# A fused attention and gated convolution kernel: tail emitted by a list schedule, padded tiles, z in halves, the remainder's bank emptied by one copy

## Chip, cores and metric

The kernel runs on one core of a Trainium2 chip. The metric is the device time of one execution in microseconds; the profile comes from one profiled execution. Engines are named as in the profile: PE is TensorE, PEld its weight loads, DVE is VectorE, ACT is ScalarE, POOL is GpSimd, SP is SyncE, which here only issues DMAs.

## Reference

```python
scores = (1.0 / S) * np.matmul(z, z.transpose(0, 2, 1))      # z: 4 x 3136 x 64
attn = np.maximum(scores, 0.0) ** 2
x = u * np.matmul(attn, v)                                   # u, v: 4 x 3136 x 256
h = np.maximum(x @ w_in, 0.0)                                # w_in: 256 x 1024
hp = h padded by one row of zeros at both ends of the sequence
conv_out = sum(conv_w[k] * hp[:, k:k + S, :] for k in range(3))
gate = 1.0 / (1.0 + np.exp(-conv_out))
out = h * gate @ w_out                                       # w_out: 1024 x 256
```

## The kernel before

Four batches are cut into six blocks of 512 rows of the sequence each, 24 blocks in all, and a remainder of 64 rows per batch. A block takes 25 slots; a slot is one chunk of 128 keys. `scores` multiplies za and zb (z and its low part, both as fp32r) into a PSUM bank "s"; ScalarE applies the relu, ScalarE or VectorE squares, ScalarE casts to fp32r (tile ah), VectorE subtracts for the rest (tile al), and that frees the bank. `attend` accumulates ah and al with v into the two banks av0 and av1. Because scores are symmetric, part of them is not computed again: they are written to DRAM as 16-bit halves by `part` and `spill`, fetched transposed and put together on GpSimd by `join` (tiles tp, tj). In every product both operands are split in a high and a low part, and three matmuls are made of one.

While block n is in attention, block n - 1 goes through the second part, one hidden chunk (128 of 1024 hidden columns, 8 chunks a block) at a time: `ffn_in` makes six matmuls from xh and xl into a bank "ph"; ScalarE applies the relu into the SBUF tile hb (three buffers, with two columns of the neighbour block ahead: `ffn_halo`), and multiplies by the first tap; VectorE adds two taps (`ffn_conv`); ScalarE takes the sigmoid, VectorE gates, ScalarE casts to gh, GpSimd subtracts for gl; `ffn_out` makes two triples of matmuls (lines 584 to 586) into o0 and o1. The eight PSUM banks are two "s", two "ph", av0, av1, o0 and o1.

The order of work is a table of slots: `at(slot, class, function)` puts a step into a class of a slot, and a loop over the slots emits them. Every engine then works through its own queue in that order. In the tail, behind the last slot, the last block's eight chunks and the eight chunks of the joined remainder of all batches (256 rows, tile hr, 266 columns with the seams) follow in pairs with fixed offsets (`T_M`, `T_R`, `T_O`, in `last_block`); the last block uses banks "ph" and collects in av0 and av1, the remainder uses "s" and collects in o0 and o1.

The remainder's attention of a batch is made by `rem_fetch`, `rem_join` (GpSimd), `rem_square` (VectorE), `rem_split`, and `rem_attend`, which accumulates into the bank av0 at the head of the batch's last block but one. `rem_evac` empties av0: ScalarE casts it, VectorE subtracts from it; only then av0 is free for the block. z is prepared by `prep_z` for 512 columns at a time: a cast on ScalarE (za), one on VectorE (zb), two subtractions on GpSimd.

Of the kernel before, what the change touches and what calls it, by code (L numbers as in the profile page):

```python
# [55 lines left out]
T_X = 0  # L56
T_O = [1, 1, 1, 2, 2, 2, 3, 3]
T_C = [3, 3, 3, 3, 1, 1, 2, 1, 2]
T_H, T_L = "AAVAAVAA", "GVGVGVGV"
T_M = [0, 2, 4, 6, 8, 10, 12, 14]  # L60
T_R = [1, 3, 5, 7, 9, 11, 13, 15]
T_P, T_E, T_RO = {4: 0, 5: 0, 6: 1, 7: 4}, 5, 6
# [5 lines left out]
def kernel(  # L68
# [90 lines left out]
    def part_z(c, t, hi, lo):  # L159
        (e0, e1), (e2, e3) = hi, lo  # L160
        copy(e0, za[LO, c], t[LO])
        copy(e1, zb[HI, c], t[HI])
        sub(e2, zb[LO, c], t[LO], za[LO, c])
        sub(e3, za[HI, c], t[HI], zb[HI, c])

    def prep_z(q, cast=None):
        c, t = slice(q * NB, min((q + 1) * NB, S)), zst.pop(q)
        g = nc.gpsimd
        part_z(c, t, (cast or nc.scalar, nc.vector), (g, g))
# [314 lines left out]
    def gate_x(blk, eng):  # L484
        t, o = ut[blk], pav.pop(blk)
        nc.vector.scalar_tensor_tensor(
            out=t[:, 0], in0=o[0], scalar=SCALE, in1=t[:, 0], op0=ALU.mult, op1=ALU.mult
        )
        x = wk.tile([P, NB], F32, tag="x1", name="x1", bufs=1)
        nc.scalar.mul(x, o[1], SCALE)  # L490
        eng.tensor_tensor(out=t[:, 1], in0=x, in1=t[:, 1], op=ALU.mult)

    def split_x(blk, engs):
        t = ut.pop(blk)
        xh[blk] = wk.tile([P, DC, NB], F32R, tag="xh", name="xh", bufs=1)
        xl[blk] = wk.tile([P, DC, NB], F32R, tag="xl", name="xl", bufs=1)
        for dc in range(DC):
            nc.scalar.copy(xh[blk][:, dc], t[:, dc])
            sub(engs[dc], xl[blk][:, dc], t[:, dc], xh[blk][:, dc])

# [9 lines left out]
    def ffn_in(blk, f, tag="ph"):  # L510
# [12 lines left out]
    def ffn_halo(blk, f):  # L523
# [5 lines left out]
        t = wk.tile([P, NB + 2], F32, tag="hb", name="hb", bufs=3)  # L529
# [6 lines left out]
    def ffn_relu(blk, f):  # L536
# [4 lines left out]
        nc.scalar.activation(t[:, 2:], p, AF.Relu)  # L541
        b, q = divmod(blk, QB)
        nc.gpsimd.tensor_copy(halo[:, f] if q < QB - 1 else ends[:, f, b], t[:, NB:])  # L543
# [35 lines left out]
    def ffn_out(blk, f, dc, tag="o"):  # L579
        if f == 0 and dc == 0:  # L580
# [11 lines left out]
    def outs(blk):  # L592
        r = ob[blk]
        if blk == "r":
            r = r.rearrange("p a (b n) -> p a b n", b=B)
            return [
                (out[b, :, QB * NB - 1 :].rearrange("(a p) s -> p a s", p=P), r[:, :, b, : RQ + 1]) for b in range(B)
            ]
# [3 lines left out]
        return [(out[b, :, t + a : t + NB].rearrange("(a p) s -> p a s", p=P), r[:, :, a:])]  # L602

    def evac(blk, end=False):
        e = width(blk)
        o = po.pop(blk)
        if blk == "r":
            r = wk.tile([P, DC, RW], F32, tag="ut", name="ob", bufs=1)
        else:
            r = wk.tile([P, DC, NB], F32, tag="ob", name="ob", bufs=1)  # L610
        ob[blk] = r
        for dc in range(DC):
            if end and dc:
                nc.vector.tensor_copy(r[:, dc, :e], o[dc][:, :e])
            else:
                nc.scalar.copy(r[:, dc, :e], o[dc][:, :e])
        if end:
            for dst, src in outs(blk):
                for dc in range(DC):
                    (nc.scalar if dc else nc.sync).dma_start(out=dst[:, dc], in_=src[:, dc])  # L620

    def store(blk):
        for dst, src in outs(blk):
            nc.sync.dma_start(out=dst, in_=src)
# [14 lines left out]
    for q in range(2, QB + 1):  # L639
        s = 4 * q - LA - 3 if q < QB else 4 * QB - LA - 4  # L640
        at(max(s - 4, -LA), POST, load_z, 0, q)
        at(s, POST, prep_z, q)
    at(-3, POST, prep_z, 1)
# [5 lines left out]
    for b in range(1, B):  # L649
        k0 = (b * QB - 1) * NJ  # L650
        for q in range(QB + 1):
# [10 lines left out]
            at(s, POST, prep_z, q)  # L662
# [7 lines left out]

    n = len(RN) - 1
    for b in range(B):
# [11 lines left out]
        at(k5 + 1, PRE, rem_evac)  # L684
        at(k5 + R_T, PE1, rem_turn)
# [12 lines left out]

    for blk in range(NBLK - 1):
# [3 lines left out]
        ahead = blk == NBLK - 2  # L703
        for f in range(FC):
            s = k0 + FS[f]
            at(s, POST, ffn_halo, blk, f)
            at(s, PE1, ffn_in, blk, f)
            at(s + RELU, C_RELU, ffn_relu, blk, f)
            at(s + TAP, C_TAP, ffn_tap, blk, f)
            at(s + ST1, C_ST1, ffn_conv, blk, f, 1)  # L710
            at(s + ST2, C_ST2, ffn_conv, blk, f, 2)
            at(s + SIG, C_SIG, ffn_sig, blk, f)
            at(s + GATE, C_G, ffn_gate, blk, f, G)
            h = s + (GATE if ahead and f >= FC - 2 else GHI)
            at(h, C_HI, ffn_hi, blk, f, A)
            at(h, PE1, ffn_lo, blk, f, G)
            o0, o1 = s + OUT0, s + OUT1
            if ahead and f in T_P:
                o0 = o1 = NS + T_P[f]
            at(o0, PE0, ffn_out, blk, f, 0)  # L720
            at(o1, PE0, ffn_out, blk, f, 1)
        e = NS + T_E if ahead else s + EVAC
        at(e, C_EV, evac, blk)
        at(e + 1, POST, store, blk)

    def last_block():
        blk = NBLK - 1
        at(NS, PRE, gate_x, blk, V)
        at(NS + T_X, T_C[0], split_x, blk, (V, V))
        at(NS - 2, POST, rem_x)  # L730
        jobs = [(NS + T_M[f], blk, f, "ph", "av") for f in range(FC)]
        jobs += [(NS + T_R[f], "r", f, "s", "o") for f in range(FC)]
        for s, w, f, tag, to in sorted(jobs, key=lambda x: x[0]):
            r, t, s1, s2, g, m, h, l = (s + x for x in T_O)
            at(s, POST, ffn_halo, w, f)
            at(s, PE1, ffn_in, w, f, tag)
            at(r, T_C[1], ffn_relu, w, f)
            at(t, T_C[2], ffn_tap, w, f)
            at(s1, T_C[3], ffn_conv, w, f, 1)
            at(s2, T_C[4], ffn_conv, w, f, 2)  # L740
            at(g, T_C[5], ffn_sig, w, f)
            at(m, T_C[6], ffn_gate, w, f, E[T_L[f]])
            at(h, T_C[7], ffn_hi, w, f, E[T_H[f]])
            at(l, T_C[8], ffn_lo, w, f, E[T_L[f]])
            o = s + 4 if w != "r" else max(s + 4, NS + T_RO)
            at(o, PE0, ffn_out, w, f, 0, to)
            at(o, PE0, ffn_out, w, f, 1, to)
            if f == FC - 1:
                at(o, PE1, evac, w, True)

    last_block()
# [5 lines left out]
    with tc.manual_schedule():  # L757
# [11 lines left out]
        rem_picks()  # L769
        nc.sync.dma_start(out=craw.bitcast(U64), in_=conv_w.rearrange("p f k -> p (f k)"))  # L770
        for k in range(-LA, max(ev) + 1):
# [77 lines left out]
```

## Time and profile before

| what | value |
|---|---|
| median of 3 runs | 1627.96 us (1625.5 to 1630.11) |
| profiled execution | 1626.88 us |
| its span in the profile | 1624.8 us |
| PE, DVE, ACT, POOL busy | 97%, 70%, 76%, 68% |

The span is from the first to the last instruction that the profile shows; 2.1 us of the execution lie around it. A share of busy time is a mean over stages with different limits.

### The profile page before, as it was taken

The numbers are of one execution on the slowest core, as the hardware profiler recorded it, in microseconds if no ns is written. First come the engines' busy times: TensorE is split into PE (matmuls) and PEld (weight loads), VectorE is DVE, ScalarE is ACT, GpSimd is POOL, SyncE is SP. The second block draws the span as 40 slices with busy tenths as digits, with TensorE's granted clock in tenths as the row PEclk, the third lists the DMA queues.
The fourth block names the chain that finished last, engine by engine and source line by source line (L and its number), as shares of the span: only waits on it lengthen the run. The fifth ranks groups of instructions, "written<-read, shape, count | busy, mean of one in ns | idle before, by whom it ended". The sixth has DMA issues, their size and how long they took to land.

```text
span 1624.8 us, 22336 instructions
## 1 busy us (share of the span) xinstructions
PE 1578.1 (97%) x6868; PEld 1277.0 (79%) x6868; DVE 1133.4 (70%) x1712; ACT 1232.6 (76%) x2299; POOL 1106.9 (68%) x1320
## 2 busy tenths in 40 slices
PE   7999999999999999999999999999999999999986
PEld 5667888778888888878888888887888888887874
DVE  7787676666777766666777776666677776666566
ACT  7888777778777777868877777777877777786764
POOL 6766557877866766778776676777775666677632
PEclk9999999999999999999999999999999999999999
DMA  4342334545435445446343444454543444545400
GB/s 143 109 129 69 114 84 108 128 99 131 135 88 136 106 89 133 106 114 141 94 139 95 117 119 109 103 122 96 141 134 90 121 91 102 122 102 121 104 20 20
DMA packets 352921, 175.70 MB, mean 108 GB/s; under 512 B 260640, under 2 KB 337440, under 8 KB 352800
## 3 DMA queue, kind: packets, MB, share of 16 engines
q1 hardware_dynamic: 352080, 173.88, 42.4%
q8 instruction: 53, 0.87, 0.2%
q14 instruction: 68, 0.56, 0.1%
q10 hardware_dynamic: 720, 0.40, 0.1%
HBM read 36.59 MB, written 75.24 MB: 69 GB/s over the span
## 4 chain that ended last, share of the span: by engine, by line
PE 80%; ACT 7%; DVE 5%; POOL 4%; issue 3%; DMA 1%; SPq 0%; ACTq 0%; POOLq 0%; DVEq 0%
PE av L380 41%; PE ph L517 5%; PE ph L515 5%; PE ph L516 5%; PE o L586 5%; PE o L584 5%; PE o L585 5%; PE s L288 5%; PE s L289 4%; DVE ph L553 2%; PE av L445 1%; POOL tj L332 1%; ACT t L340 1%; ACT ph L548 1%; DVE al L144 1%
## 5 line engine op out<-in xcount | busy, mean ns | idle before, releaser
L380 PE MATMUL av<-ah,vv 128*128 128x512 f32 x2400 | 742.5, 392 | 6.6 <-DVE ar L144 3.0
L144 DVE TENSOR_TENSOR al<-s,ah 128x512 fp32r<-128x512 f32 x576 | 397.2, 690 | 220.5 <-ACT ah L356 158.5
L380 PEld LDWEIGHTS av<-ah,vv 128*128 128x128 f32 x2400 | 449.5, 188 | 113.5 <-DVE ar L144 4.7
L380 PE MATMUL av<-al,vv 128*128 128x512 f32 x1152 | 451.7, 392 | 3.7 <-DVE al L144 3.4
L351 DVE TENSOR_TENSOR s<-s,t 128x512 f32<-128x512 f32 x345 | 240.6, 697 | 182.2 <-ACT t L340 180.3
L340 ACT ACTIVATE t<-s 128x512 f32<-128x512 f32 x372 | 222.6, 598 | 115.7 <-PE s L289 102.4
L332 POOL COPY tj<-tp 128x1024 uint16<-128x1024 uint16 x228 | 307.9, 1360 | 0.4
L358 ACT CAST ah<-s 128x512 fp32r<-128x512 f32 x372 | 218.8, 588 | 104.6 <-DVE s L351 103.4
L553 DVE SCALAR_TENSOR_TENSOR ph<-hb,cw,ph 128x512 f32<-128x512 f32 x384 | 286.8, 747 | 12.5 <-ACT ph L548 11.9
L144 POOL TENSOR_TENSOR gl<-hb,gh 128x512 fp32r<-128x512 f32 x188 | 243.4, 1294 | 59.2 <-ACT gh L147 54.8
L308 POOL COPY pl<-t 128x1024 uint16<-128x1024 uint16 x248 | 259.1, 1050 | 9.0 <-DMA dq<-pl 8.6
L380 PEld LDWEIGHTS av<-al,vv 128*128 128x128 f32 x1152 | 216.6, 188 | 54.0 <-DVE al L144 9.1
L543 POOL COPY halo<-hb 128x2 f32<-128x2 f32 x160 | 31.5, 197 | 220.8 <-ACT hb L541 219.7
L288 PE MATMUL s<-za 128*128 128x512 f32 x372 | 148.0, 398 | 18.2 <-DVE al L144 12.6
L584 PE MATMUL o<-gh,wol 128*128 128x512 f32 x384 | 153.4, 399 | 3.7 <-ACT gh L147 2.5
L560 ACT ACTIVATE ph<-ph 128x512 f32<-128x512 f32 x200 | 115.6, 578 | 54.6 <-DVE ph L553 48.6
L586 PE MATMUL o<-gl,woh 128*128 128x512 f32 x384 | 153.0, 399 | 4.1 <-POOL gl L144 2.9
L515 PE MATMUL ph<-xh,wih 128*128 128x512 f32 x384 | 150.4, 392 | 2.4 <-DVE hb L567 2.4
L585 PE MATMUL o<-gh,woh 128*128 128x512 f32 x384 | 152.2, 396 | 0.0
L517 PE MATMUL ph<-xl,wih 128*128 128x512 f32 x384 | 150.9, 393 | 1.0 <-DVE xl L144 0.7
L337 ACT ACTIVATE s<-tj 128x512 f32<-128x512 f32 x228 | 136.7, 600 | 18.8 <-POOL tj L332 18.5
L516 PE MATMUL ph<-xh,wil 128*128 128x512 f32 x384 | 150.3, 391 | 0.0
(118 smaller groups left out, 2117.5 us busy)
## 6 DMA issues: line engine op xcount, KB each, us to landing
dq<-pl SPq DMA_DIRECT2D x228, 256.0 KB, 2.4
vst<-in_v_dram SPq DMA_DIRECT2D x48, 256.0 KB, 3.2
ut<-in_u_dram SPq DMA_DIRECT2D x24, 512.0 KB, 4.3
out_dram<-ob SPq DMA_DIRECT2D x19, 512.0 KB, 3.7
st<-in_z_dram SPq DMA_DIRECT2D x24, 256.0 KB, 3.0
tp<-dq SPq DMA_TRANSPOSE x228, 3.5
dq<-pl SPq DMA_DIRECT2D x20, 128.0 KB, 2.5
wr<-in_moe_w_in_dram SPq DMA_DIRECT2D x8, 256.0 KB, 3.1
```

Of the source, the lines that this page charges most:

```text
L144: eng.tensor_tensor(out=out, in0=a, in1=b.bitcast(F32), op=ALU.subtract)
L308: nc.gpsimd.tensor_copy(pl[k], rl.pop(k).bitcast(U16).rearrange("p (n h) -> p h n", h=2))
L332: nc.gpsimd.tensor_copy(tj[k].bitcast(U16).rearrange("p (n h) -> p h n", h=2), t)
L340: nc.scalar.activation(rl[k], sc[k][:, :NB], AF.Relu, scale=SC1)
L351: nc.vector.tensor_tensor(out=s, in0=s, in1=rl[k], op=ALU.mult)
L380: nc.tensor.matmul(o, lhsT=w[:, j, d], rhs=r, start=first and i == 0, stop=last and i == len(ops) - 1)
L515: nc.tensor.matmul(o, lhsT=wih[:, dc, w], rhs=xh[blk][:, dc], start=(dc == 0), stop=False)
L517: nc.tensor.matmul(o, lhsT=wih[:, dc, w], rhs=xl[blk][:, dc], start=False, stop=(dc == DC - 1))
L553: nc.vector.scalar_tensor_tensor(out=c, in0=hb[blk, f][:, k : e + k], scalar=cw[:, f, k : k + 1], in1=c, op0=ALU.mult, op1=ALU.add,)
L584: nc.tensor.matmul(o, lhsT=wol[:, f, d], rhs=h, start=(f == 0), stop=False)
L585: nc.tensor.matmul(o, lhsT=woh[:, f, d], rhs=h, start=False, stop=False)
L586: nc.tensor.matmul(o, lhsT=woh[:, f, d], rhs=l, start=False, stop=(f == FC - 1))
```

## The change

- The tail (`tail`, in place of `last_block`) is a list of operations with fixed costs and dependencies, ordered by a list schedule and then emitted in that order. The last steps of the block before (chunks 4 to 7) are part of the list. Chunks alternate between banks "s" and "ph" in pairs, all casts are on ScalarE, the subtractions of the last block on GpSimd, those of the remainder on VectorE. Both halves of the last gate are on VectorE. The remainder is stored with one DMA per half instead of four.
- The tile hb has 528 words a row instead of 514. In the program's layout the three buffers of hb stood 2,080 bytes apart, 6,240 in all, so that gh and gl behind them began at 205,536 and 211,680, which is 32 past a multiple of 64. Now the buffers stand 2,112 bytes apart, and gh and gl begin at 199,488 and 205,632, multiples of 64. The tiles ah, al, xh, xl, za and vv begin at multiples of 64 in both.
- `prep_z` has two halves (za cast and its subtraction; zb cast and its subtraction). From the second batch on the second half is two slots later. The zb cast is on ScalarE for odd chunks of columns.
- `rem_evac` copies av0 to an SBUF tile on ScalarE and casts from there; the subtraction (`rem_low`) is on GpSimd, four slots later. `rem_square` is on ScalarE.
- The matrix `pick` (`rem_picks`) is made at slot 100 instead of ahead of the loop. `ffn_in` takes the two matmuls with xl last.

```diff
-    def prep_z(q, cast=None):
-        c, t = slice(q * NB, min((q + 1) * NB, S)), zst.pop(q)
+    def prep_z(q, half):
...
+        if half == 0:
+            copy(nc.scalar, za[LO, c], t[LO])
+            sub(g, zb[LO, c], t[LO], za[LO, c])
+            return
+        copy(nc.scalar if q % 2 else nc.vector, zb[HI, c], t[HI])
+        sub(g, za[HI, c], t[HI], zb[HI, c])
...
     def rem_square(i):
         t = rs[i]
-        nc.vector.scalar_tensor_tensor(out=t, in0=t, scalar=1.0 / SC1, in1=t, op0=ALU.mult, op1=ALU.mult)
+        nc.scalar.activation(t, t, AF.Square, scale=SC1**-0.5)
...
-        nc.scalar.copy(h, o)
-        sub(nc.vector, l, o, h)
+        rr["t"] = t = wk.tile([P, NB], F32, tag="t", name="re", bufs=3)
+        nc.scalar.copy(t, o)
+        nc.scalar.copy(h, t)
+
+    def rem_low():
+        sub(nc.gpsimd, rr["l"], rr.pop("t"), rr["h"])
...
             nc.tensor.matmul(o, lhsT=wil[:, dc, w], rhs=xh[blk][:, dc], start=False, stop=False)
+        for dc in range(DC):
             nc.tensor.matmul(o, lhsT=wih[:, dc, w], rhs=xl[blk][:, dc], start=False, stop=(dc == DC - 1))
...
-        t = wk.tile([P, NB + 2], F32, tag="hb", name="hb", bufs=3)
+        t = wk.tile([P, NB + 16], F32, tag="hb", name="hb", bufs=3)
...
+            at(s, POST, prep_z, q, 0)
+            at(s + 2, POST, prep_z, q, 1)
...
+    at(4 * NJ, POST, rem_picks)
...
+        at(k5 + 5, POST, rem_low)
...
+        def ffn(w, f, stage, x, tag, eh, el, to):
+            n, r = width(w), w == "r"
+            a, v = 90 + 0.82 * n, 60 + 1.07 * n
...
+                d = op("P", 2.5 * (n + 32), x + hold(tag, 2), ffn_in, w, f, tag)
+                d = op("A", a, [d, d0], ffn_relu, w, f)
...
+                d = op("A", a + 100, [d], ffn_tap, w, f)
+                d = op("V", v, [d], ffn_conv, w, f, 1)
+                d = op("V", v + 100, [d], ffn_conv, w, f, 2)
...
+        free, done, order = defaultdict(float), {}, []
+        while len(order) < len(ops):
...
+                t = max([free[e]] + [done[d] + 35 for d in deps])
+                k = (t, -rank[i])
...
+        for i in order:
+            ops[i][3](*ops[i][4])
```

On ScalarE in the tail, before: two pairs of the last block (hb, 512 columns) and the remainder (hr, 256 or 266 columns). L541 and L539 are the relu, L548 the tap, L560 the sigmoid, L147 the cast; the number behind ph is that of the chunk's bank tile.

```order
L541 ACTIVATE hb_16802<-ph_16810 128x512
L548 ACTIVATE ph_16810<-hb_16802,cw_73 128x512
L560 ACTIVATE ph_16810<-ph_16810 128x512
L539 ACTIVATE hr_16828<-ph_16837 128x4x64
L548 ACTIVATE ph_16837<-hr_16828,cw_73 128x266
L147 CAST gh_16869<-hb_16802 128x512
L560 ACTIVATE ph_16837<-ph_16837 128x266
L541 ACTIVATE hb_16854<-ph_16862 128x512
```

The same engine in the tail after the change, where L552 and L550 are the relu, L562 the tap, L574 the sigmoid, L144 the cast.

```order
L552 ACTIVATE hb_16621<-ph_16664 128x512
L550 ACTIVATE hr_16640<-ph_16678 128x4x64
L562 ACTIVATE ph_16664<-hb_16621,cw_73 128x512
L562 ACTIVATE ph_16678<-hr_16640,cw_73 128x266
L574 ACTIVATE ph_16643<-ph_16643 128x266
L144 CAST gh_16710<-hb_16593 128x512
L552 ACTIVATE hb_16686<-ph_16699 128x512
L574 ACTIVATE ph_16664<-ph_16664 128x512
L562 ACTIVATE ph_16699<-hb_16686,cw_73 128x512
```

Before, the sigmoid of a chunk stands right behind its tap. After, four rows of other chunks stand between the tap and the sigmoid of ph_16664.

On GpSimd, ahead of the second batch, before: two chunks of z (za, zb) among joins (tj), subtractions for gl and halo copies.

```order
L543 COPY halo<-hb 128x2
L144 TENSOR_TENSOR zb<-st,za 64x512
L144 TENSOR_TENSOR za<-st,zb 64x512
L144 TENSOR_TENSOR zb<-st,za 64x512
L144 TENSOR_TENSOR za<-st,zb 64x512
L332 COPY tj<-tp 128x2x512
L144 TENSOR_TENSOR gl<-hb,gh 128x512
```

The same place after the change.

```order
L557 COPY halo<-hb 128x2
L141 TENSOR_TENSOR zb<-st,za 64x512 x2
L328 COPY tj<-tp 128x2x512
L141 TENSOR_TENSOR gl<-hb,gh 128x512
L544 COPY hb<-halo 128x2
L328 COPY tj<-tp 128x2x512
L141 TENSOR_TENSOR za<-st,zb 64x512 x2
```

Two of the four subtractions have moved behind the next two joins.

## Rows read from the trace of the kernel before

**Rows 1.** Windows: busy us (instructions) of PE, PEld, DVE, ACT, POOL; clock; DMA.

```profile
60.00:1559.00 1499.00, 1481.35 (x6461) 1204.99 (x6461) 1045.64 (x1568) 1151.69 (x2134) 1046.86 (x1226) 1.00 0.44 111
1559.00:1625.00 66.00, 47.86 (x224) 36.48 (x222) 40.56 (x70) 35.70 (x73) 15.92 (x45) 0.95 0.07 21
```

**Rows 2.** The chain that ended last, one pair of the tail: start, us, what.

```profile
1593.03 0.70 ACT ph L548
...
1593.76 0.77 DVE ph L553
...
1595.34 0.58 ACT ph L560
...
1596.31 0.50 ACT ph L548
...
1598.87 0.70 ACT ph L548
```

**Rows 3.** Groups of the tail (1559:1625): busy us, mean ns, idle before, its releasers.

```profile
L560 ACT ACTIVATE ph<-ph 128x512 f32<-128x512 f32 x10 | 5.8, 580 | 11.6 <-DVE ph L553 11.6
...
L553 DVE SCALAR_TENSOR_TENSOR ph<-hb,cw,ph 128x512 f32<-128x512 f32 x18 | 13.5, 754 | 9.9 <-ACT ph L548 9.7
...
L144 POOL TENSOR_TENSOR gl<-hb,gh 128x512 fp32r<-128x512 f32 x7 | 8.9, 1278 | 16.5 <-ACT gh L147 12.2 <-DVE gh L147 4.3
```

**Rows 4.** Timeline of PE, two stretches of the tail: start, us, instruction.

```profile
1559.23 0.39 PE L515 MATMUL ph<-xh,wih 128*128 128x512 f32 x1
...
1560.59 0.40 PE L584 MATMUL o<-gh,wol 128*128 128x512 f32 x1
...
1563.41 0.40 PE L515 MATMUL ph<-xh,wih 128*128 128x512 f32 x1
...
1608.64 0.28 PE L515 MATMUL ph<-xr,wih 128*128 128x256 f32 x1
...
1609.23 0.28 PE L517 MATMUL ph<-xr,wih 128*128 128x256 f32 x1
```

**Rows 5.** Timeline of the end, PE's last matmul and SP's last issues.

```profile
1618.40 0.28 PE L586 MATMUL o<-al,woh 128*128 128x266 f32 x1
...
1617.92 3.38 SPq L620 DMA_DIRECT2D out_dram<-ob  x5
```

**Rows 6.** DMA issues of the end: KB each, median us to landing.

```profile
out_dram<-ob SPq DMA_DIRECT2D x4, 32.5 KB, 2.4
```

**Rows 7.** Waits of PE, 60:1559: us in total, times, longest us.

```profile
PE s L288 <- DVE al L144: 12.6, 11, 2.8
PE av L380 <- DVE ar L144: 3.0, 4, 0.8
```

**Rows 8.** Timeline where the remainder's bank is emptied, second batch: ACT, DVE, PE.

```profile
727.73 0.59 ACT L456 CAST ar<-av 128x512 fp32r<-128x512 f32 x1 [5.31 <-PE av L445]
...
728.35 0.69 DVE L144 TENSOR_TENSOR ar<-av,ar 128x512 fp32r<-128x512 f32 x1 [6.12 <-ACT ar L456]
...
729.09 0.50 PE L380 MATMUL av<-ah,vv 128*128 128x512 f32 x1 [0.75 <-DVE ar L144]
```

**Rows 9.** Timeline of POOL and PE, z prepared ahead of the second batch.

```profile
279.48 1.29 POOL L144 TENSOR_TENSOR zb<-st,za 64x512 fp32r<-64x512 f32 x1 [1.16 <-DVE zb L147]
...
284.92 1.34 POOL L332 COPY tj<-tp 128x1024 uint16<-128x1024 uint16 x1
...
288.70 0.50 PE L288 MATMUL s<-za 128*128 128x512 f32 x1 [2.39 <-DVE al L144]
```

**Rows 10.** Timeline of DVE and PE, squares of the first batch's remainder.

```profile
318.22 1.74 DVE L431 SCALAR_TENSOR_TENSOR rj<-rj 128x512 f32<-128x512 f32 x1 [2.51 <-POOL rj L410]
...
326.18 0.50 PE L288 MATMUL s<-za 128*128 128x512 f32 x1 [2.79 <-DVE al L144]
```

**Rows 11.** Timeline of DVE and PE at the start.

```profile
8.12 1.24 DVE L394 CAST pick<-pk 128x64 fp32r<-128x64 f32 x1 [2.11 <-POOL pk L391]
...
10.74 0.77 PE L380 MATMUL av<-ah,vv 128*128 128x512 f32 x1 [1.81 <-ACT ah L358]
```

More of the change, by code (lines that the diff above doesn't have):

```diff
@@ L157, in load_z @@
         zst[q] = t[:, :w]
[L159 to L164, printed above, removed]
-    def prep_z(q, cast=None):
-        c, t = slice(q * NB, min((q + 1) * NB, S)), zst.pop(q)
-        g = nc.gpsimd
-        part_z(c, t, (cast or nc.scalar, nc.vector), (g, g))
+    def prep_z(q, half):
+        c = slice(q * NB, min((q + 1) * NB, S))
+        t = zst.pop(q) if half else zst[q]
+        g = nc.gpsimd
+        if half == 0:
[4 more added lines that the diff above has]
+        sub(g, za[HI, c], t[HI], zb[HI, c])
         if q == QB:
@@ L540, in ffn_relu, with ffn_keep @@
             return
-        nc.scalar.activation(t[:, 2:], p, AF.Relu)
+        nc.scalar.activation(t[:, 2 : NB + 2], p, AF.Relu)
+    def ffn_keep(blk, f):
+        t = hb[blk, f]
         b, q = divmod(blk, QB)
-        nc.gpsimd.tensor_copy(halo[:, f] if q < QB - 1 else ends[:, f, b], t[:, NB:])
+        nc.gpsimd.tensor_copy(halo[:, f] if q < QB - 1 else ends[:, f, b], t[:, NB : NB + 2])
     def ffn_tap(blk, f):
@@ L579, in ffn_out @@
     def ffn_out(blk, f, dc, tag="o"):
-        if f == 0 and dc == 0:
+        if blk not in po:
             po[blk] = [ps.tile([P, 512], F32, tag=f"{tag}{i}", name=f"o{i}") for i in range(DC)]
@@ L601, in outs, with evac, store_half @@
         t = q * NB - 1
-        return [(out[b, :, t + a : t + NB].rearrange("(a p) s -> p a s", p=P), r[:, :, a:])]
-    def evac(blk, end=False):
+        return out[b, :, t + a : t + NB].rearrange("(a p) s -> p a s", p=P), ob[blk][:, :, a:]
+    def evac(blk, dcs=range(DC), engs=(nc.scalar, nc.scalar)):
         e = width(blk)
-        o = po.pop(blk)
-        if blk == "r":
[L608 to L620, printed above, removed]
+        if blk not in ob:
+            if blk == "r":
+                ob[blk] = wk.tile([P, DC, RW], F32, tag="ut", name="ob", bufs=1)
+            else:
+                ob[blk] = wk.tile([P, DC, NB], F32, tag="ob", name="ob", bufs=1)
+        for dc in dcs:
+            copy(engs[dc], ob[blk][:, dc, :e], po[blk][dc][:, :e])
+    def store_half(blk, dc, eng):
+        if blk == "r":
+            dst = out[:, dc * P : (dc + 1) * P, QB * NB - 1 :].rearrange("b p s -> p b s")
+            eng.dma_start(out=dst, in_=ob[blk][:, dc].rearrange("p (b n) -> p b n", b=B)[:, :, : RQ + 1])
+            return
+        dst, src = outs(blk)
+        eng.dma_start(out=dst[:, dc], in_=src[:, dc])
     def store(blk):
-        for dst, src in outs(blk):
-            nc.sync.dma_start(out=dst, in_=src)
+        dst, src = outs(blk)
+        nc.sync.dma_start(out=dst, in_=src)
     ev = defaultdict(lambda: tuple([] for _ in range(6)))
@@ L697, with before_end @@
         at(blk * NJ + 6, POST, load_u, blk)
+    def before_end(slot, *args):
+        if slot < NS:
+            at(slot, *args)
     for blk in range(NBLK - 1):
@@ L702 @@
         at(k0 + XS, C_XS, split_x, blk, (G, G))
-        ahead = blk == NBLK - 2
         for f in range(FC):
             s = k0 + FS[f]
+            if s == NS - 1:
+                break
             at(s, POST, ffn_halo, blk, f)
@@ L711 @@
             at(s + ST2, C_ST2, ffn_conv, blk, f, 2)
[L712 to L749, printed above, removed]
@@ L768 @@
         prep_v(0, V)
-        rem_picks()
         nc.sync.dma_start(out=craw.bitcast(U64), in_=conv_w.rearrange("p f k -> p (f k)"))
-        for k in range(-LA, max(ev) + 1):
+        for k in range(-LA, NS):
             e = ev[k]
@@ L807 @@
                 run(e[PE1])
+        tail()
 _INS = ['u', 'v', 'z', 'moe_w_in', 'moe_conv_w', 'moe_w_out']
```

132 lines of the change are left out of this document (107 added, 25 removed).

## Prediction

> **What bounds the kernel now.** I read the stages first. From 60 to 1559 us TensorE is busy 1481.35 of 1499 us, while ScalarE, VectorE and GpSimd are busy about 70 to 77% [rows 1]. So the body runs at TensorE's own rate, and an edit there counts only where TensorE waits or where its matmuls get shorter. After the last attention matmul, at about 1559.0, the picture changes: in 66 us TensorE works 47.86, VectorE 40.56 and ScalarE 35.70 [rows 1]. Nothing is full, so the tail is bound by order. The chain of waits shows which: one pair (a chunk of the last block, then a chunk of the remainder) runs from 1593.03 to 1598.87, 5.84 us, through ScalarE's tap, two convolution steps on VectorE, the sigmoid, then the same for the remainder, and only then the next tap [rows 2]. The groups of the tail say the same: ScalarE waits 11.6 us in front of the sigmoid for VectorE, VectorE waits 9.9 us in front of the convolution for ScalarE [rows 3]. The two engines take turns.
>
> The profiled execution took 1626.88 us, 1.1 below the median of the three; I make the sum against it.
>
> **The tail's order.** In the new order ScalarE has two or three rows of other chunks between a tap and the sigmoid that waits for VectorE behind it, so the turns overlap. What remains is the largest load. For TensorE I count it: 54 matmuls of 512 columns into the hidden chunks at 0.227 us (six in 1.36 us, [rows 4]) are 12.3 us; 72 out of them, at 0.235 now (twelve in 2.82 us, [rows 4]) and 0.227 if the next part holds, are 16.9 or 16.3; 48 of 256 columns at 0.118 (five steps in 0.59 us, [rows 4]) are 5.7; 48 of 266 columns, by columns 0.123, are 5.9. Sum 40.2. ScalarE takes four casts more, at most 0.6 each like the one in [rows 8], and stays under 38.1; VectorE gives those up and trades four subtractions of 512 columns for four of 266, so it is below its 40.56; GpSimd has some ten subtractions of 1.28 us [rows 3]. So TensorE becomes the bound, with VectorE close behind. A slot of PSUM does not hold it up: a chunk of the last block may start when the second one before it is gated, and 1.36 + 0.58 + 0.70 + 2 x 0.77 + 0.58 + 0.70 = 5.5 us [rows 2] (relu and gate taken like the sigmoid and the tap) for two pairs is 2.8 a pair against TensorE's 4.2 (two sets of 1.4, one of 0.7, one of 0.74). Waits are left: the end (the last remainder chunk has some 4 us of elementwise work, of which the outputs of the two last chunks and of two remainder chunks, 4.3 us, cover most) and places where the tail's in-order queues meet VectorE late. Between nothing and 8 us (one more microsecond a pair) I take 3.
>
> Behind the last matmul the end took 1624.8 - 1618.40 = 6.4 us. Four small stores per half become one: SyncE's five issues took 3.38 us, 0.68 each [rows 5], and one of the small stores landed 2.4 us after its issue [rows 6]. One issue in place of four saves up to 2.0 on that queue; as the joined store has four times the pieces I take back a little and count 1.6 saved, 4.8 left. The tail then ends at 1559.0 + 40.2 + 3.0 + 4.8 = 1607.0 instead of 1624.8: **-17.8 us** (-12 with the 8 us of waits and a store that gains nothing, -20 with 1 us of waits).
>
> **The padded tiles.** The triple that multiplies by the output weights steps at 0.235 us, the triple ahead of it at 0.227, both with 512 columns, 128 rows and the same clock [rows 4]. What differs is where the moving tile lies: only gh and gl begin 32 bytes past a multiple of 64; after the padding they begin on one. [...] That the address is the cause is inferred from two groups of rows, no run here shows it yet. 1152 such matmuls, less the 72 already counted, times 0.0075 to 0.008 are 8.1 to 8.6 us of a body in which TensorE is 99% busy. Some will come back as waits, since others must keep up: I take **-7**, between 0 and -8.6.
> The Trainium skill's page "TensorE: Matmul & The Clock Gate", section "Back-to-back issue gap", speaks against this edit: it gives the spacing of warm matmuls as columns / 2.4 + 2.5 ns, 215.8 ns for 512, with no term for an address. By that page the padding changes nothing. Neither of the two spacings in the rows is the page's, and they differ from each other, so I go by the rows.
>
> **The remainder's bank.** Four times, once a batch, TensorE waits for the accumulator of the remainder, 3.0 us in all [rows 7]. ScalarE copies it at 727.73 for 0.59, then VectorE subtracts at 728.35 for 0.69, and the matmul starts at 729.09 [rows 8]. After the change the bank is free when the copy ends, 728.32, so it starts about 0.7 earlier. ScalarE then has one more cast (0.59) in front of the next attention cast, which was needed only after two matmuls and an output triple. 4 x 0.6 = **-2.4** (bounds -0.4 and -3.0). The subtraction moves to GpSimd four slots later, ahead of the turn at slot 13, which leaves it several slots.
>
> **z in halves and the squares.** The other waits of the body are those of the scores for VectorE's subtraction, which frees their bank: 12.6 us in 11 places [rows 7]. Two have a cause that the change touches. At 279.48 four z subtractions of 1.29 stand in a row on GpSimd ahead of a join at 284.92, and TensorE then waits 2.39 at 288.70 [rows 9]; in the new order two stand there and two behind the next two joins. That is 2.7 us less ahead of the first join, so the wait can go whole; I take 2.0, as the other pair now delays a later join. At 318.22 VectorE's square waits 2.51 for GpSimd and then takes 1.74; TensorE waits 2.79 at 326.18 [rows 10]. On ScalarE the nearest row, a copy of 512 columns, is 0.59 [rows 8], so 1.15 is gained and VectorE is no longer held behind that wait; but ScalarE is now held instead. I take 2.0 over all four batches (bounds +2 and -4). The zb casts that go to ScalarE (odd chunks) lie in its idle 23%; they would cost where it is already late. Together **-4** (bounds 0 and -6.4).
>
> **The start.** VectorE waits 2.11 for the pick matrix and spends 1.24 on it at 8.12, and the first attention matmul starts at 10.74 after a wait for what comes behind it [rows 11]. That work moves to slot 100, long before the matrix is first used. ScalarE gets one cast of z more there (0.6 at most). 1.81 of wait, less that: **-1.2** (bounds 0 and -1.8).
>
> **At nothing:** the order of the six input matmuls (the first of them in a block waits for its tile, the others have it), the second gate half on VectorE, the earlier list positions of halo copies.
>
> Sum: 17.8 + 7 + 2.4 + 4 + 1.2 = 32.4, so 1626.9 - 32.4 = **1594.5 us**, 2.0% faster. With the parts at their better and worse ends together about 1588 to 1603; that is this case's own range.
>
> **Rivals.** *The address is not the cause.* Then the spacing of the output triples stays 0.235: -7 and the 0.5 in the tail fall away, 1602 us. For it: no row shows the same tile at another address, and by the page above this is what should come out. Against it: ah, al, xh, xl and za all step at 0.227, and the two groups of rows have nothing else apart but weights that are laid out alike.
>
> *The tail stays a chain.* The new order was made with fixed costs per operation; if one engine is late, every in-order queue behind it is, and when TensorE waits long its clock may be granted at half, as the mean of 0.95 for the tail hints [rows 1]. At 5.3 us a pair in place of 5.84 and the shorter end, the tail gains about 6 us: 1626.9 - 6 - 14.6 = 1606 us. Against it: in the new order no pair of rows that wait for each other stand next to each other on ScalarE until the last chunks.
>
> *Squares that hold ScalarE.* Sixteen squares now stand in ScalarE's queue, each behind a join on GpSimd; behind it wait the relu, the casts and so every engine. VectorE's wait at 318.22 was 2.51 [rows 10]. If each of the sixteen held TensorE for that long, it would cost 40 us and the kernel would end at 1626.9 - 30.4 + 40 = 1637, slower. It decides from 30.4 / 16 = 1.9 us a square. Against it: the body's eleven waits of this kind come to 12.6 us in all, so most of the sixteen joins were not late; joins are also relieved of z work.
>
> **Chances.** The sum as worked out 0.62; the address not the cause 0.18; the tail a chain 0.15; squares that decide 0.05. A difference of 0.3%, about 5 us, is what this kernel's runs can tell from none. The first three are all faster; I leave 0.93 for faster, 0.02 for the same and 0.05 for slower, as the three could meet. For 8 in 10 the range goes from 1588 to 1607, which takes in the two middle rivals.
>
> **What would show it.** Right: output triples at 0.227 in the body; the four waits for the remainder gone to 0.1 or so; no wait of over 1 us at the place of 288.70; in the tail TensorE busy nearly throughout at full clock, from the last attention matmul to the last output in some 43 us; first attention matmul near 9.5. Wrong: triples still at 0.235; ScalarE waiting for GpSimd in front of the squares with the scores late behind it; pairs in the tail over 5 us apart with ScalarE and VectorE still waiting for each other.

## The result and the profile after

The changed kernel takes 1600.25 us (median of 4 runs, 1598.48 to 1600.64), the kernel before 1628.47 us: ratio 0.9827, 95% interval 0.981 to 0.9844. The forecast was 1594.5 us with a range of 1588 to 1607. The profiled execution took 1600.44 us, its span is 1598.67; before it was 1626.88 and 1624.85. The sums by place below are made with the profiled executions, 26.2 us of span apart.

Two rows of the windows of after (window, its length, busy us and count of PE, PEld, DVE, ACT, POOL; granted clock; share and GB/s of the DMA), cut at the last attention matmul, answer to [rows 1]:

```profile
60.00:1552.00 1492.00, 1483.13 (x6455) 1202.93 (x6454) 1017.13 (x1538) 1164.25 (x2161) 1044.36 (x1231) 1.00 0.45 111
1552.00:1599.00 47.00, 41.62 (x222) 34.87 (x221) 35.06 (x66) 34.71 (x75) 17.93 (x45) 0.98 0.09 29
```

The body takes 7.4 us less: the last attention matmul starts at 1551.60 where it started at 1559.01. Of that, 2.4 us are won up to the first attention matmul of the third block (136.56 in place of 138.99) and 5.0 behind it. The tail behind it goes from 65.8 us to 47.07 (1551.60 to the span's end at 1598.67), with TensorE busy 41.62 of it.

**The tail's order.** The first and the last of the sixteen taps (eight chunks of the last block, eight of the remainder) in ScalarE's timeline (start, us, instruction), in before and then in after, answer to the pairs of [rows 2]:

```profile
1566.71 0.69 ACT L548 ACTIVATE ph<-hb,cw 128x512 f32<-128x512 f32 x1
...
1614.49 0.49 ACT L548 ACTIVATE ph<-hr,cw 128x266 f32<-128x266 f32 x1
```

```profile
1558.46 0.69 ACT L562 ACTIVATE ph<-hb,cw 128x512 f32<-128x512 f32 x1
...
1588.95 0.49 ACT L562 ACTIVATE ph<-hr,cw 128x266 f32<-128x266 f32 x1
```

The eight pairs took 47.8 us, 6.0 each; here they take 30.5, 3.8 each. The two kinds of chunk no longer alternate strictly, so only this mean can be compared. The groups of the tail in after (busy us, mean ns of one, idle time before and who ended it) answer to [rows 3]:

```profile
L567 DVE SCALAR_TENSOR_TENSOR ph<-hb,cw,ph 128x512 f32<-128x512 f32 x18 | 13.5, 752 | 3.3 <-ACT ph L562 3.0
...
L574 ACT ACTIVATE ph<-ph 128x512 f32<-128x512 f32 x9 | 5.2, 581 | 2.3 <-DVE ph L567 2.2
```

ScalarE's 11.6 us of waiting in front of the sigmoid are 2.3, VectorE's 9.9 in front of the convolution 3.3: the two no longer take turns. The end in after, its last matmul and SyncE's first store there, then the row of the DMA issues for one half of the remainder's output (KB, us to landing), answers to [rows 5, 6]:

```profile
1591.43 0.34 SPq L628 DMA_DIRECT2D out_dram<-ob  x1
...
1593.82 0.28 PE L600 MATMUL o<-al,woh 128*128 128x266 f32 x1
```

```profile
out_dram<-ob SPq DMA_DIRECT2D x1, 130.0 KB, 2.3
```

From the last matmul to the end it is 4.85 us, 6.45 before.

**The body's waits.** The waits of PE in after from 60 to 1552 us (total, times, longest) answer to [rows 7]:

```profile
PE s L284 <- DVE al L141: 5.6, 7, 1.8
...
PE ph L528 <- POOL xl L141: 0.8, 4, 0.2
```

The scores' waits fell from 12.6 to 5.6 us. The four waits for the remainder's bank are gone from the list, and four others stand in it that were not there.

The timeline of after where the bank is emptied answers to [rows 8]:

```profile
720.92 0.59 ACT L453 COPY re<-av 128x512 f32<-128x512 f32 x1 [5.31 <-PE av L441]
721.54 0.62 ACT L454 CAST ar<-re 128x512 fp32r<-128x512 f32 x1
721.56 0.30 PEld L376 LDWEIGHTS av<-ah,vv 128*128 128x128 f32 x2 [0.45 <-ACT re L453]
...
724.25 1.14 ACT L144 CAST xh<-ut 128x512 fp32r<-128x512 f32 x2
724.94 2.54 POOL L141 TENSOR_TENSOR xl<-ut,xh 128x512 fp32r<-128x512 f32 x2 [8.24 <-ACT xh L144]
...
727.53 0.50 PE L528 MATMUL ph<-xl,wih 128*128 128x512 f32 x1 [0.20 <-POOL xl L141]
```

The bank is free at 721.51 and the matmul goes on at once. (This is the head of the sixth and last block of a batch, where the remainder's attention stands, and not of the last but one.) But the second cast on ScalarE, 0.62, stands ahead of the cast of xh, then GpSimd makes xl, and the second of the hidden chunk's matmuls with xl waits for that.

**z and the squares.** The timeline of after at the places of [rows 9, 10]:

```profile
277.39 2.55 POOL L141 TENSOR_TENSOR zb<-st,za 64x512 fp32r<-64x512 f32 x2 [1.16 <-ACT za L144]
279.87 1.35 POOL L328 COPY tj<-tp 128x1024 uint16<-128x1024 uint16 x1
...
284.14 2.54 POOL L141 TENSOR_TENSOR za<-st,zb 64x512 fp32r<-64x512 f32 x2
...
284.68 0.50 PE L284 MATMUL s<-za 128*128 128x512 f32 x1 [0.41 <-DVE al L141]
```

The wait of 2.39 is 0.41; the one of 2.79 at 326.18 has no successor. The block in which both lie (the fifth, from its first attention matmul to that of the sixth) takes 67.7 us, 72.7 before: 5.0 gained.

**The output triples.** One triple and the matmuls behind it (a row x2 holds two), in after and then in before, answer to [rows 4]; the last row of each is the tenth matmul:

```profile
600.88 0.39 PE L598 MATMUL o<-gh,wol 128*128 128x512 f32 x1
601.11 0.39 PE L599 MATMUL o<-gh,woh 128*128 128x512 f32 x1
601.34 0.39 PE L600 MATMUL o<-gl,woh 128*128 128x512 f32 x1
601.58 0.62 PE L376 MATMUL av<-ah,vv 128*128 128x512 f32 x2
...
602.96 0.62 PE L376 MATMUL av<-ah,vv 128*128 128x512 f32 x2
```

```profile
599.53 0.40 PE L584 MATMUL o<-gh,wol 128*128 128x512 f32 x1
...
601.61 0.39 PE L288 MATMUL s<-za 128*128 128x512 f32 x1
```

The triple steps at 0.233, not at 0.227, and the matmuls behind it are slow too: nine take 2.08 us, where 9 x 0.227 is 2.04. In before the nine took 2.08 as well. Averaged over the nines without a wait from 150 to 1535 us they take 2.075 us in before and 2.080 in after. Nothing came of the padding.

### The profile page after: what moved, and what is told of

The parts are those of the page before. It is cut to its first block, busy times and chain, and to the rows that moved or that the text cites. A ratio compares the mean times of both kernels' runs of the same rounds, so it can differ in the third digit from the quotient of the medians.

```text
span 1598.7 us, 22354 instructions
## 1 busy us (share of the span) xinstructions
PE 1576.5 (99%) x6868; PEld 1275.3 (80%) x6868; DVE 1098.3 (69%) x1676; ACT 1247.7 (78%) x2334; POOL 1108.2 (69%) x1324
## 4 chain that ended last, share of the span: by engine, by line
PE 85%; ACT 6%; DVE 4%; POOL 3%; issue 2%; DMA 0%; POOLq 0%; DVEq 0%; ACTq 0%
PE av L376 43%; PE o L600 5%; PE o L599 5%; PE o L598 5%; PE ph L528 5%; PE ph L525 5%; PE ph L526 5%; PE s L284 5%; PE s L285 5%; PE av L441 1%; POOL tj L328 1%; POOL xl L141 1%; ACT t L336 1%; DVE ph L567 1%; DVE al L141 1%
## 5 line engine op out<-in xcount | busy, mean ns | idle before, releaser
L141 POOL TENSOR_TENSOR gl<-hb,gh 128x512 fp32r<-128x512 f32 x192 | 248.5, 1294 | 55.0 <-ACT gh L144 54.5
L285 PE MATMUL s<-za,zb 128*128 128x512 f32 x372 | 146.4, 393 | 0.0
L552 ACT ACTIVATE hb<-ph 128x512 f32<-128x512 f32 x192 | 114.6, 597 | 37.8 <-PE ph L528 37.1
```

Source lines behind the costliest of these rows:

```text
L141: eng.tensor_tensor(out=out, in0=a, in1=b.bitcast(F32), op=ALU.subtract)
```

## The experiments

Times are medians, to be held against 1600.25 of after. In one place the clock disturbs comparisons of 1 or 2 us: in after it was granted at half, the lower level (1.2 GHz), for 3.4 us from 95.4 us on, behind a wait of 1.81; in *old_evac* (below), with the same wait at 94.73, it was not. The row of each:

```profile
95.40:99.00 3.60, 3.55 (x9) 2.80 (x10) 3.28 (x7) 1.44 (x3) 1.02 (x2) 0.53 0.55 152
```

```profile
94.40:98.00 3.60, 3.27 (x14) 2.71 (x15) 3.37 (x7) 2.50 (x6) 1.74 (x4) 1.00 0.51 152
```

From the second block's first attention matmul to the third's that makes 1.6 us (72.2 and 70.6 us). The profiled executions of after, before, unpadded, operands, low_tiles, squares_dve and picks_early have it, the others not, and after's median holds it, as by their mean clocks three of its four runs do. So where it matters I compare the stretch from the third block's first attention matmul to the last attention matmul, 1415.0 us in after; of these profiles only operands and z_whole have a half clock inside it.

**old_tail**: the kernel after, with the old tail (the slots of its table, its emptying of the banks and its stores).

```diff
...
-    tail()
+    last_block()
```

> All edits of the change except the tail: the tail of before stands behind the new body. If the tail's gain is its own (66 us shrank to 47 after the last attention matmul), this kernel loses about 18.8 us against the changed one, some 1619 us, and its body, from the start to the last attention matmul, is as long as that of the changed kernel, 1551.6 us in the span. If the rival holds, that the new body brings the tail's engines to the end in a better state, the old tail is shorter here than 65.8 us and the kernel ends near 1610.

Measured: 1618.36 us, 0.9947 of before (0.9932 to 0.9962). The new tail is worth 18.1 us, as the prediction's term; by the profiles the tail behind the last attention matmul is 65.30 us here and 47.07 in after, 18.2 apart. The old tail is nearly as long as in before, 65.84, so the new body does not shorten it. The body ends 2.0 us earlier than after's, for the most part since the half clock at 95 us is lacking.

**unpadded**: hb of 514 words again.

```diff
-        t = wk.tile([P, NB + 16], F32, tag="hb", name="hb", bufs=3)
+        t = wk.tile([P, NB + 2], F32, tag="hb", name="hb", bufs=3)
```

> The changed kernel with hb of 514 words again, so that gh and gl lie 32 past a multiple of 64. My term for the padding says 7 us slower, 1607, with output triples 8 ns a matmul longer than those of the changed kernel. The rival, read from the trace of the changed kernel (its triples still step at 0.233 us, and attention matmuls behind them are longer by 1 to 3 ns than before), says that the padding is worth nothing or a small loss: 1597 to 1602, triples at 0.235.

Measured: 1598.05 us (1596.55 to 1599.48), span 1597.4 against 1598.7. The padding wins nothing; by the profiles, with the same half clock in both, it loses 1.3. The nine matmuls show why: 2.075 us here on average, 2.080 in after, and there are 384 of them, up to 2 us in all.

**operands**: the triples of the first output half take other weights, those of the second half z as their moving tile.

```diff
...
+        if blk != "r" and dc == 0:
+            wa, wb = wil[:, 0, f * P : (f + 1) * P], wih[:, 0, f * P : (f + 1) * P]
+        if blk != "r" and dc == 1:
+            h, l = za[:, :NB], za[:, NB : 2 * NB]
...
```

> The changed kernel with other operands in the output triples, so the output is not the reference's: for the first half of the columns the weights are taken from the input weights, for the second half the moving tile is z. It asks what makes output triples step at 0.233 us where all other matmuls of 512 columns step at 0.227. If it is the address or the content of the moving tiles gh and gl, the first half stays at 0.233 and the second falls to 0.227. If it is the weights' place, the first half falls and the second stays. If it is the PSUM bank, both stay.

Measured: 1601.35 us in one run. Its timeline, a triple of each half:

```profile
602.09 0.39 PE L603 MATMUL o<-gh,wil 128*128 128x512 f32 x1
...
604.17 0.39 PE L284 MATMUL s<-za 128*128 128x512 f32 x1
...
604.62 0.39 PE L603 MATMUL o<-za,wol 128*128 128x512 f32 x1
...
606.66 0.62 PE L376 MATMUL av<-ah,vv 128*128 128x512 f32 x2
```

Nine matmuls from a triple on take 2.08 us with gh and other weights, 2.04 with z and the old weights. So it is the moving tile, neither the weights nor the bank, and the slow steps of the attention matmuls behind it go with it. In the blocks where z is prepared that gain is lost: in the fifth the triples wait 3.1 us for the writing of za, with a stretch of half clock from 277.1 us on, so it gains 0.7 us on before, where after's gains 5.0, and in the ninth and the fifteenth they wait 0.9 each. The other 19 blocks from the third on take 5.0 us less than in after: half the triples, and half of what *in_phase* (below) gains there.

**low_tiles**: gh and gl at another place.

```diff
+        for n in ("gh", "gl"):
+            nc.vector.memset(wk.tile([P, NB], F32R, tag=n, name=n, bufs=3)[:, 0:1].bitcast(F32), 0.0)
         load_z(0, 0)
```

> The kernel after the change, but the six tiles of gh and gl are set aside first of the work pool, so that they lie at byte 128832 to 141119 of a partition in place of 199488 to 211775; what came before them moves up by 12 KB, with xh at 197248 and xl at 201344, inside the old range. If the place in SBUF makes the slow steps, the output triples go from 0.233 us to 0.227 and the six matmuls behind them from 1.381 to 1.362; xl, now where gh was, may go to 0.233. Then 384 triples gain 0.038 us each, 14 us, less 384 x 0.006 for xl: 1588 us. If what the tiles hold makes it, the triples stay at 0.233, xl at 0.227, and the time stays at 1600.

Measured: 1600.6 us, the nine still 2.08. Not the place as such; but the new address is as far past a multiple of 512 bytes as the old one (320), which I saw only later.

**plain_data**: other contents in gh and gl of all blocks, not in the remainder's.

```diff
-        copy(eng, g[0], cc[blk, f])
+        if blk == "r":
+            copy(eng, g[0], cc[blk, f])
+        else:
+            copy(eng, g[0], wih[:, 0, :NB].bitcast(F32))
```

> The kernel after the change, but the cast into gh reads 512 columns of the input weights in place of the gated chunk, so that gh and gl hold numbers of the size of the weights (some 0.06) and not those of the hidden chunk; the output is not the reference's. Instructions, addresses and waits stay. If what the tiles hold makes the slow steps, the output triples go to 0.227 us and the attention matmuls behind them to 0.227 as well, and the kernel to about 1586. If the place makes them, all steps stay as they are, at 1600.

Measured: 1598.55 us in one run, without the half clock at 95 us; a triple and the tenth matmul:

```profile
599.29 0.39 PE L601 MATMUL o<-gh,wol 128*128 128x512 f32 x1
...
601.37 0.62 PE L376 MATMUL av<-ah,vv 128*128 128x512 f32 x2
```

The nine take 2.08 us with numbers of another size: not the contents.

**align128**: hb of 544 words.

```diff
-        t = wk.tile([P, NB + 16], F32, tag="hb", name="hb", bufs=3)
+        t = wk.tile([P, NB + 32], F32, tag="hb", name="hb", bufs=3)
```

> The kernel after the change, with hb tiles of 544 words in place of 528, so that gh and gl begin on a multiple of 128 bytes; after the change they begin 64 bytes past one, before it 96 bytes past one, and so they still did in the run with gh and gl at a low place. All other moving tiles (ah, al, xh, xl, za) begin on a multiple of 128, and they step at 0.227 us. If the address within 128 bytes makes the slow steps, the output triples go to 0.227 us and the six attention matmuls behind each to 1.362 from 1.381: 384 times 0.038 us, 14 us less, 1586. If not, and only the sort of tile or its writers count, 1600.

Measured: 1598.54 us (1598.49 to 1601.21), no gain beyond the half clock, which its profiled execution lacks. The steps moved, though:

```profile
598.73 0.40 PE L598 MATMUL o<-gh,wol 128*128 128x512 f32 x1
598.97 0.39 PE L599 MATMUL o<-gh,woh 128*128 128x512 f32 x1
599.19 0.40 PE L600 MATMUL o<-gl,woh 128*128 128x512 f32 x1
...
600.81 0.62 PE L376 MATMUL av<-ah,vv 128*128 128x512 f32 x2
```

On average the triple steps at 0.234, 0.225 and 0.237 in place of three times 0.233, and the nine are 2.08 as ever. The address shapes how the loss is spread, and a multiple of 128 is not the cure.

**shift_ah**: 64 bytes ahead of all that follows ah.

```diff
...
+            zst["pad"] = wk.tile([P, 16], F32, tag="pad", name="pad", bufs=1)
...
         ah[k] = wk.tile([P, NB], F32R, tag="ah", name="ah", bufs=4)
```

> The kernel after the change, with 64 bytes set aside ahead of the ring of ah, so that all that comes after it moves up by 64 bytes: ah, al, xh and xl then begin 64 bytes past a multiple of 128, gh and gl on one. If the address within 128 bytes makes the slow steps, the output triples go to 0.227 us and the attention matmuls, the hidden chunks' matmuls go to about 0.233: some 5300 attention matmuls of 512 columns and 1150 of the hidden chunks lose 0.006 us each, 39 us, less 14, so 1625. If not, all steps stay as they are, 1600.

Measured: 1611.78 us in one run, 11.5 slower than after; without the early half clock, from the third block to the last attention matmul, 1428.3 us against 1415.0, 13.2 slower. From 150 to 1540 us the attention matmuls step at 0.232 on average and the hidden chunks' at 0.230. (The trace has 3552 attention matmuls, not the 5300 of the expectation, whose 39 us become 28.) The scores' matmuls, whose tile za had not moved, went from 0.227 to 0.237 and 0.229, and the triples, though on a multiple of 128 now, stayed slow; as slow steps run on for some five matmuls, both could come from the tiles ahead of them.

One reading is that a tile is slow only beside tiles that begin at another offset. The long runs of attention matmuls speak against it. Nine matmuls in the midst of 18 that read ah and al alone, here and then in after:

```profile
323.25 0.63 PE L380 MATMUL av<-ah,vv 128*128 128x512 f32 x2
...
325.36 0.40 PE L529 MATMUL ph<-xh,wih 128*128 128x512 f32 x1
```

```profile
323.75 0.61 PE L376 MATMUL av<-ah,vv 128*128 128x512 f32 x2
...
325.79 0.39 PE L525 MATMUL ph<-xh,wih 128*128 128x512 f32 x1
```

They take 2.11 us here and 2.04 in after. All these tiles have one offset in either kernel; in after the steps are back at 0.227 from the sixth matmul of such a run on, here they are still 0.232 at the eighteenth (means of 16 runs). And the 25 matmuls of a batch's remainder that read vv, set aside with za and not moved, are back at 0.227 from the sixth on in this kernel too. So a common offset is not enough: the offset itself counts. By the addresses of the compiled programs, bytes past a multiple of 512:

| kernel | za | ah, al, xh, xl | gh, gl | nine matmuls, us |
|---|---|---|---|---|
| before, unpadded | 128 | 128 | 224 | 2.08 |
| after, plain_data, low_tiles | 128 | 128 | 320 | 2.08 |
| align128 | 128 | 128 | 0 | 2.08 |
| shift_ah | 128 | 192 | 384 | 2.09 |
| operands, second half | 128 | 128 | za in their place | 2.04 |

**in_phase**: gh and gl set aside in hi_half, behind xl, so that they too begin 128 past a multiple of 512.

```diff
+        if blk == 0 and dc == 0:
+            for n in ("gh", "gl"):
+                nc.gpsimd.memset(wk.tile([P, NB], F32R, tag=n, name=n, bufs=3)[:, 0:1].bitcast(F32), 0.0)
```

> The kernel after the change, but the rings of gh and gl are set aside right behind xl, ahead of hb, so that gh begins at byte 193152, which is 128 past a multiple of 512, as are the beginnings of all moving tiles that step at 0.227 us (za 16512, ah 156288, al, xh, xl). In the kernel after the change gh begins 320 past such a multiple, in the run with the low place 320 too, in before 224 and in the run with tiles of 544 words 0, and in each of these an output triple and the six matmuls behind it took 2.075 to 2.080 us in place of 9 x 0.227 = 2.043. If the phase of the address within 256 or 512 bytes makes it, all nine go to 0.227, and 384 times 0.037 us are won: 14 us, 1586. If another thing of gh and gl makes it (that they are newly written, their ring), the nine stay at 2.08 and the time at 1600.

Measured: 1586.95 us (1586.26 to 1588.58, 5 runs), 0.9756 of before (0.9742 to 0.9769). It beats both kernels. A triple, and the next triple nine matmuls on:

```profile
600.64 0.39 PE L601 MATMUL o<-gh,wol 128*128 128x512 f32 x1
600.87 0.39 PE L602 MATMUL o<-gh,woh 128*128 128x512 f32 x1
601.10 0.39 PE L603 MATMUL o<-gl,woh 128*128 128x512 f32 x1
601.32 0.61 PE L376 MATMUL av<-ah,vv 128*128 128x512 f32 x2
...
602.68 0.39 PE L601 MATMUL o<-gh,wol 128*128 128x512 f32 x1
```

All nine step at 0.227, 2.04 together. 384 triples at 0.037 are 14 us; the medians are 13.3 apart, but after's holds the half clock at 95 us and this one does not. From the third block to the last attention matmul it is 1403.5 us against 1415.0, 11.6 gained. A little comes back as waits: from 150 to 1535 us the scores wait 1.5 us, 0.4 in after.

**squares_dve**: the remainder's squares on VectorE again.

```diff
-        nc.scalar.activation(t, t, AF.Square, scale=SC1**-0.5)
+        nc.vector.scalar_tensor_tensor(out=t, in0=t, scalar=1.0 / SC1, in1=t, op0=ALU.mult, op1=ALU.mult)
```

> The changed kernel with the squares of the remainder on VectorE again. If these squares made the waits at 326.18 and at the same place of the other three batches (2.8 + 0.6 + 1.2 + 0.4 us, all gone after the change), they come back: about 5 us slower, 1605. If the z halves alone removed them, as they take work from GpSimd ahead of the joins, nothing changes: 1600 within 1 us.

Measured: 1603.28 us, 3.0 slower; the spans, both with the half clock, are 3.9 apart. The four blocks in which the squares stand are 1.2, 0.5, 1.0 and 0.8 us longer. The square that had waited 2.51 and taken 1.74 in [rows 10] shows why; here on VectorE, and then in after on ScalarE:

```profile
312.36 1.73 DVE L427 SCALAR_TENSOR_TENSOR rj<-rj 128x512 f32<-128x512 f32 x1 [1.65 <-POOL rj L406]
```

```profile
311.92 0.63 ACT L427 ACTIVATE rj<-rj 128x512 f32<-128x512 f32 x1 [1.02 <-POOL rj L406]
```

**z_whole**: the second half of z in the slot of the first, batches 1 to 3.

```diff
-            at(s + 2, POST, prep_z, q, 1)
+            at(s, POST, prep_z, q, 1)
```

> The kernel after the change, but z is prepared at once again, with four subtractions of 1.29 us in a row on GpSimd. By the prediction 2.0 us are lost, at the place of 284.68 in the trace of after (a wait of 0.57 there, 2.39 before): 1602. If the halves gained nothing because the second pair delays a later join as much, the time stays at 1600. If the whole gain of 5.0 between the fourth and the fifth block comes from the halves and not from the squares, 1603 to 1605.

Measured: 1602.93 us, 2.7 slower. The wait is back, and here the half clock follows it:

```profile
284.12 0.50 PE L284 MATMUL s<-za 128*128 128x512 f32 x1 [2.40 <-DVE al L141]
...
284.69 0.73 PE L376 MATMUL av<-ah,vv 128*128 128x512 f32 x2
285.22 0.63 PE L376 MATMUL av<-al,vv 128*128 128x512 f32 x1
285.65 1.05 PE L376 MATMUL av<-ah,vv 128*128 128x512 f32 x2
```

The wait of 0.41 is 2.40 again, 2.0 us, as forecast. The steps behind it are 0.427 us, at a granted clock of 0.58 from 284.5 to 288. The spans (each with one such stretch) are 1.4 apart, so the halves are worth 1.4 to 2.7, with a half clock in this kernel that may itself be a cost of the wait.

**old_evac**: the bank read by ScalarE and VectorE again; the subtraction goes back from GpSimd to VectorE with it.

```diff
-        rr["t"] = t = wk.tile([P, NB], F32, tag="t", name="re", bufs=3)
-        nc.scalar.copy(t, o)
-        nc.scalar.copy(h, t)
+        nc.scalar.copy(h, o)
+        sub(nc.vector, l, o, h)
...
```

> The kernel after the change, but the remainder's accumulator is read twice again, by the cast on ScalarE and by VectorE's subtraction, as before. By the prediction the bank comes free 0.6 us later four times: 2.4 us slower, 1602.7. By the trace of after, the wait for the bank fell from 0.91 to 0.185 us, and a wait of 0.37 for xl stands six matmuls on, where there was none; if that wait is the same delay at another place, the old way costs no more than about 0.35 x 4 = 1.4, and 1600 to 1601.5 is what is measured.

Measured: 1598.51 us (1598.19 to 1600.26); less the half clock that its profile lacks, it is level with after. Its waits at the place of [rows 8] are one:

```profile
PE av L376 <- DVE ar L141: 0.7, 1, 0.7
```

The wait for xl is not there. Matmul by matmul, after gains 0.73 us on this kernel at the bank and gives back 0.47 where xl is late. In the first three batches it gives back 0.4 more some 27 us into the block, where the weight load of a scores' matmul waits for VectorE; the row of after, whose counterpart has no wait here:

```profile
747.87 0.19 PEld L284 LDWEIGHTS s<-za 128*128 128x128 f32 x1 [0.53 <-DVE al L141]
```

Only the fourth batch keeps its 0.26. So of this edit nothing reaches the end. Whether ScalarE's cast more or GpSimd's subtraction makes that second delay, no run separates.

**picks_early**: the pick matrix at the start again, ahead of the loop over the slots.

```diff
-    at(4 * NJ, POST, rem_picks)
...
+        rem_picks()
```

> The kernel after the change, but the pick matrix is made at the start again. By the prediction 1.2 us slower, 1601.4, with the first attention matmul at 10.7 in place of 9.45. By the marks of the two traces, first attention matmul 1.29 earlier and the second block 2.4 earlier, it may be 2.4: 1602.7, where the second 1.1 belongs to the pick matrix too; it stays 1.2 if the second belongs to the halves of z.

Measured: 1600.92 us, 0.7 slower; by the spans 1.2, with the first attention matmul at 10.69 in place of 9.45. The second block starts 1.4 earlier than before without this edit, 2.4 with it; those 1.4 have another source. Up to 67 us TensorE waits 1.8 us for al in this run and in after, 3.4 in before, so VectorE is less late; that the shared zb casts of the first batch relieve it is likely, but no run separates that. (In the first batch the two halves stand in one slot; and in this run the granted clock was at half from 11.3 to 14.8 us, in after up to 13.7.)

## Why the prediction was right and where it was wrong

The time lies in the range and the tail, more than half of the sum, came out as forecast and for the reason given. Two other terms failed: the padding by 8.3 us, the remainder's bank by its 2.4. Three came out larger than reckoned, the tail by 1.0, z and the squares by 1 or more, the start by 1.2 in the first block. So the total is only 6 us off, and that these misses had opposite signs is luck.

Two bounds are added up wrongly: waits of 8 us and a store that gains nothing leave the tail a gain of 11.2 us, not 12; and the parts at their better and worse ends together make about 1587 and 1614, not 1588 and 1603.

**The tail's order** (term 17.8): measured 18.8 between the marks, 18.1 by the run that puts the old tail back. TensorE did become the bound: 42.2 us from the last attention matmul to its own last, where 40.2 of matmuls and 3 of waits were reckoned, so the waits were 2 or less. The end is 4.85, reckoned 4.8.

**The padded tiles** (term 7): this step failed. It read from [rows 4] that the triples are slow because gh and gl begin 32 bytes past a multiple of 64, and took a multiple of 64 for the cure. That the start address makes it was right, the rule for it was wrong: with gh at 320, 0 and 224 bytes past a multiple of 512 the nine stay at 2.08, at 128 all of the loss goes. I had also looked at triples alone and not at what steps behind them: the slow steps run on for some five matmuls that read well placed tiles, so the loss in before was 0.033 us a triple, 12.6 us, and not 8. The page "TensorE: Matmul & The Clock Gate" of the Trainium skill, section "Back-to-back issue gap", has no term for an address; by it the padding does nothing. That is nearly what came, but in_phase shows that an address is worth 11.6 us, so the page's rule does not hold for these matmuls. The rival "the address is not the cause" forecast 1602 and was nearest in time, for a reason that is false.

**The remainder's bank** (term 2.4): mis-sized, nothing in its place. The wait did go, 0.73 us each time, as worked out. The step that failed is the slack: what was taken as harmless, one cast more on ScalarE and a subtraction on GpSimd, comes back as 0.47 us of wait for xl and, in three batches, 0.4 for the scores' bank.

**z in halves and the squares** (term 4): mis-sized, 3.5 to 3.9 for the squares and 1.4 to 2.7 for the halves. The place of 288.70 gave the 2.0 forecast. Squares gave more, since a VectorE that waits for a join and then takes 1.7 us holds the subtraction that frees the scores' bank in all four batches. The rival of squares that hold ScalarE did not come: ScalarE waits for a join in front of four of the sixteen squares, 4.0 us together, where 40 were feared.

**The start** (term 1.2): 1.29 at the first attention matmul, 1.2 by the spans of picks_early.

Together by these runs: 18.8 + 3.9 + 1.4 + 1.2 - 1.3 (padding) = 24.0 of the 26.2 us of span; old_evac gives nothing or a little against that. Of the remaining 2, 1.2 lie in the first block (56.1 us before, 55.0 after); no run separates their cause.

## What to carry to other kernels

When two groups of equal matmuls step differently, sum the steps over the slow group and those behind it, and list the start addresses of all the tiles that TensorE streams: here the one offset that stepped fast was 128 past a multiple of 512, and an order of allocation puts a tile there at no cost. Take the rule from tiles that are known to be fast, not from a round number that fits the slow ones, and compare runs in a stretch where the clock was the same. A wait that is removed by adding an operation to another engine's queue is only gone when what stands behind that operation has slack. A tail whose engines are two thirds busy is worth an order worked out from costs: 18 us here, with no instruction made faster.

## What the runs showed of the hardware

A TensorE matmul of 512 fp32r columns stepped at 0.227 us when za, ah, al, xh, xl, gh and gl all began 128 bytes past a multiple of 512 (in_phase). With gh and gl at 0, 224 or 320 among such tiles, the triple that reads them and some five matmuls behind it stepped at 0.225 to 0.237, and cost 0.033 to 0.039 us together; that was worth 11.6 us. With ah, al, xh and xl at 192 (shift_ah) they stepped at 0.232 even in runs of eighteen, 13.2 us in all, while vv, not moved, was back at 0.227 within six. Weights, contents and the PSUM bank were tried and make no difference. Whether the period is 256 or 512 bytes, which other offsets are fast, and whether it is the offset of the moving tile alone or against that of the weights, no run here tells.

The granted clock fell to half for 3.4 us behind waits of TensorE of 1.81 to 2.40 us in some executions and not in others: steps of 0.427 us in place of 0.227, some 1.6 us each time. Of the four runs of after the one with a mean clock of 1.000 took 1598.48 us, the others, at 0.998 and 0.999, 1600.06 to 1600.64.
